# Five loads under way instead of eight, extra loads at other places, and an attention prologue in another order

## The chip, the core and the metric

The kernel runs on one core of one Trainium2 chip. The metric is the device time of one execution in microseconds (us). The core has five engines with a queue of instructions each: TensorE (PE, matmuls, with PEld for its weight loads), VectorE (DVE), ScalarE (ACT), GpSimd (POOL) and SyncE (SP). Here POOL issues nearly all loads, and SP the stores and the DMA transposes. An engine works through its instructions in the order in which the program has them, and waits on semaphores for what others produce.

## What is computed

```python
scores = (q @ k.T) / 8                       # 8 batches, 8 heads, 576 tokens, 64 columns a head
cum = cumsum(max(s, 0))                      # along the tokens
scores = where(causal, -1e9, scores + min(-(cum_i - cum_j), 0))
x = softmax(scores) @ v                      # to [8, 576, 512]
h = relu(x.T @ w_tok1) @ w_tok2              # mixes tokens, 256 hidden
u = x + h.T
out = u + relu(u @ w_ch1) @ w_ch2            # mixes channels, 1536 hidden
```

## The kernel before

The work goes batch by batch. A batch has two *quads* of four heads. For a quad, k and q are loaded with a cast to bf16 into a buffer of the ring `qkn` (five buffers), turned by PE (`tr`, L689), copied to `kT` and `qT` by ACT or DVE (L699, L701), multiplied into scores (L731), put through exp on ACT (L739) to `E`, masked on DVE (L748), and multiplied with v (L802); L831 and L835 divide by the row sums and write `x`. The bias of the reference is not added to the scores: its part that depends on the row cancels in the softmax, and the rest, a weight for each column token, is multiplied into v beforehand (`merge_v`, L631, by POOL or DVE). That weight `wT` comes from a running sum of s on DVE (`tensor_tensor_scan`, L534), an exp on ACT (L540) and a transpose on PE (L560).

Then `tok` mixes tokens (L899, L961) and writes `u` (L968), and turns it to `uT`: on PE for batches 0 and 1, by DMA transposes on SP from batch 2 on (L977). `chan` mixes channels: L1017 with the first weight, a relu on ACT or DVE (L1024, L1026), L1042 with the second, the sum with `u` (L1050) and the store on SP (L1055). While PE is at the channels of batch b, scores of batch b+1 run between.

Batch 0 is different: its causal mask is put into PSUM by a matmul of the identity with a mask (`preset`, L722) before the scores are added, where later batches mask `E` on DVE. Its first quad is loaded by SP without a cast (L518) and cast on ACT and DVE.

The order on the engines isn't written by hand. Every piece of work is an operation with engines that can do it, times, a priority and dependencies; `Plan.run` places them one after another by estimated times, and the program is emitted in the order of the planned starts. After it, `zero` matmuls (L1135) fill planned waits of PE in the first 45 us. A wait or an estimate that changes in one place can so move instructions in others.

All loads on POOL form one chain, in the order in which `load_op` is called, and the plan lets eight be under way:

```python
        if len(sent) >= 8:
            o.deps.add(sent[-8])
```

In the kernel before, POOL waits in the trace for a load to land when eight others are on their way. The order of the loads is: k and q of quad (0, 4), four pieces of v of batch 0, four loads of token weights, four of the first channel weight, quad (1, 0), two of the second channel weight, quad (1, 4), two more of the second channel weight, five pieces of v of batch 1, then for batches 2 to 7 a quad, v, and the other quad. After them come four quads that are loaded a second time: batches 0 and 1, for which only the sum of squares of q and k is taken on ACT (L647, `stage_sq`). These squares, with other sums, decide at the very end whether a slower general path runs; with these inputs it doesn't.

Of the kernel before, what the change touches and what calls it, by code (L numbers as in the profile page):

```python
# [8 lines left out]
FP32 = mybir.dt.float32  # L9
# [2 lines left out]
ALU = mybir.AluOpType  # L12


SWITCH = 0.095
STEADY = 50.0
MARGIN = 0.5
# [37 lines left out]
class Plan:  # L55
# [11 lines left out]
    def op(self, alts, reads=(), writes=(), prio=0, dma=0.0, holds=(), after=None, mode=0, lock=False, alone=None):  # L67
        o = Op()
        o.alts = alts
        o.prio = prio  # L70
        o.dma = dma
        o.mode = mode
        o.lock = lock
        o.alone = alone
        o.idx = len(self.ops)
        o.deps = set()
        o.users = []
        o.bufs = []
# [24 lines left out]
        self.ops.append(o)  # L103
        return o

    def run(self, eps=0.03):
# [11 lines left out]
        for o in ops:  # L118
            if o.nd == 0:
                for e in o.alts:  # L120
                    cands[e].append(o)
        dma_free = 6.0
        mode = 0
        order = []

# [17 lines left out]
        while left:  # L143
# [224 lines left out]
def kernel(  # L368
# [80 lines left out]
    chain = []  # L449
    sent = []  # L450

    def load_op(fn, key, us, occ=0.75, prio=-1):

        o = P.op({"POOL": (occ, 0, fn)}, writes=key, prio=prio, dma=us, after=chain[-1] if chain else None)
        if len(sent) >= 8:
            o.deps.add(sent[-8])
        sent.append(o)
        chain.append(o)

    def load_cast(n, b, h, i, src):  # L460
        def load():
            nc.gpsimd.dma_start(  # L462
                out=n.t[:, i, :, :],
                in_=src[b, h : h + 4, :, :].rearrange("(f e) (p r) d -> (e p) f (r d)", e=2, r=R))
        load_op(load, [(n, i)], 1.45, prio=-1 if b or h else -3)

    qkn = {}

# [47 lines left out]
    for ti, src in enumerate((k, q)):  # L516
# [4 lines left out]
        for f in range(2):  # L521
# [12 lines left out]
    P.op({"DVE": (1.3, 1.6, lambda: nc.vector.tensor_tensor_scan(  # L534
        out=cum[:, :], data0=one_sb[:, :], data1=s_sb[:, :], initial=0.0, op0=ALU.mult, op1=ALU.add))},
        reads=["sr"], writes=["cum"], prio=-1)
# [62 lines left out]
    def stage_v(b, cs=tuple(range(NJ))):  # L599
# [4 lines left out]
        for c in cs:  # L604
# [13 lines left out]
            load_op(load, [(vf, c)], 1.15 * n / 128, 0.92)  # L618
        if b:
            merge_v(b, cs)  # L620

# [50 lines left out]
    def quad(b, h):  # L672
# [4 lines left out]
        for ti in range(2):  # L677
# [6 lines left out]
            def tr(ti=ti, pv=pv):  # L684
                for r in range(R):
                    for e in range(2):
                        p0 = e * PR
                        for f in range(2):
                            nc.tensor.transpose(out=pv(e)[f * D : f * D + D, r * PR : (r + 1) * PR],  # L689
                                                in_=nat.t[p0 : p0 + PR, ti, f, r * D : (r + 1) * D],  # L690
                                                identity=ident[p0 : p0 + PR, p0 : p0 + PR])
            P.op({"PE": (R * 0.031, R * 0.031 + 0.21, tr)}, reads=([(nat, ti, 0), (nat, ti, 1)] if b == 0 and h == 0 else [(nat, ti)]) + ["ident"] + pads,
                 writes=[(pts[e], e) for e in range(2)], holds=[d[ti] for d in dsts], prio=(np_ - 30 * (b < 1 and h < 1), 2), mode=1)
# [13 lines left out]
    def pair(b, h, kT, qT):  # L707
# [3 lines left out]
        for pc, piece in enumerate(PIECES):  # L711
# [7 lines left out]
            if b == 0:  # L719
                def preset(ps=ps, pc=pc):  # L720
                    for hh in range(2):
                        nc.tensor.matmul(out=ps.t[:, hh * 512 : hh * 512 + 512], lhsT=ident[:, :], rhs=neg[:, pc, :],  # L722
                                         start=True, stop=False)
                P.op({"PE": (2 * c_pe(512)[0], 2 * c_pe(512)[0] + 0.21, preset)}, reads=["neg", "ident"],
                     writes=[(ps, 0)], prio=(np_ - 9, 0))

            def mm(ps=ps, cols=cols):
# [111 lines left out]
        P.op(dve(640, nrm), reads=[(pas[0], 0), (pas[1], 1), (rc, 0)], writes=[(x, h), (x, h + 2)], prio=0)  # L839

    def load_w(fn, key, us, occ=0.75):
        load_op(lambda: nc.gpsimd.dma_start(**fn()), [key], us, occ)
# [341 lines left out]
```

## Time and profile before

| | |
|---|---|
| Time, median of three runs | 304.92 us (304.0 to 306.28) |
| Time of the profiled execution | 306.06 us, span of its instructions 304.3 us |
| PE busy | 291.8 us (96%), granted clock 0.995 |
| ACT, DVE, POOL busy | 182.8, 172.0, 107.6 us |
| DMA | 39.29 MB moved, mean 129 GB/s |
| DMA queue of POOL's loads | 24.25 MB; of SP's transfers 14.44 MB |
| Chain that ended last | PE 84%, DMA 12% |

Times in the rows are counted from the span's start. "Busy" of PE includes the time in which a matmul drains while the next already runs, so consecutive matmuls overlap, and fillers count as work. An entry such as "[1.06 <-DMA uTb<-ub]" says that the engine was idle for 1.06 us before the instruction and that the landing of that DMA ended the wait; "issue" says that nothing in the profile did.

### The profile page before, as it was taken

How to read it: one execution, taken by the hardware profiler on the slowest of the kernel's cores; microseconds unless marked ns; L12 is line 12 of the kernel's file. 1: busy time of each engine (PE TensorE's matmuls, PEld its weight loads, DVE VectorE, ACT ScalarE, POOL GpSimd, SP SyncE). 2: the span in 40 equal slices, each digit the busy share in tenths (PEclk: the TensorE clock that was granted, in tenths of full speed). 3: DMA queues.
4: the chain of work that ended last, by engine and by line, in shares of the span. 5: the costliest groups of instructions: out<-in, count | busy, mean ns of one | idle time of the engine just before them, and what ended most of it. 6: DMA issues, size and time to landing. Idle time of an engine off the chain costs nothing.

```text
span 304.3 us, 8094 instructions
## 1 busy us (share of the span) xinstructions
PE 291.8 (96%) x3430; PEld 168.2 (55%) x3430; DVE 172.0 (57%) x368; ACT 182.8 (60%) x298; POOL 107.6 (35%) x147
## 2 busy tenths in 40 slices
PE   8899999899999999999999999998999999999991
PEld 3478566467754545457754545455764544457550
DVE  5962889377976456756556556956456642420030
ACT  5887884699996486609872387727761286017300
POOL 8675469999780418107620108500000000000000
PEclk9999999999999999999999999999999999999998
DMA  8999999999997673358455535894004310250032
GB/s 218 226 207 206 216 224 229 252 190 262 227 156 125 155 197 54 79 140 178 94 80 103 133 84 83 132 116 136 2 2 84 125 38 0 69 155 2 0 111 74
DMA packets 38348, 39.29 MB, mean 129 GB/s; under 512 B 17600, under 2 KB 30976, under 8 KB 38304
## 3 DMA queue, kind: packets, MB, share of 16 engines
q0 software_dynamic: 17072, 24.25, 44.6%
q1 hardware_dynamic: 21232, 14.44, 18.7%
q8 instruction: 29, 0.48, 0.7%
q14 instruction: 15, 0.12, 0.1%
HBM read 40.65 MB, written 9.44 MB: 165 GB/s over the span
## 4 chain that ended last, share of the span: by engine, by line
PE 84%; DMA 12%; POOL 1%; issue 1%; DVE 0%; POOLq 0%
PE pmx L1017 30%; PE pmx L1042 30%; PE pmx L961 5%; PE pmx L899 5%; PE psc L802 5%; PE psc L731 5%; DMA qkn<-in_k_dram 5%; PE psc L689 3%; DMA wc<-in_moe_w_ch_dram 3%; DMA vf<-in_v_dram 2%; DMA uTb<-us 2%; POOL qkn L462 1%; PE pmx L986 0%; DVE of L1050 0%; POOL keep masks.py:66 0%
## 5 line engine op out<-in xcount | busy, mean ns | idle before, releaser
L1017 PEld LDWEIGHTS <-wc 128*128 128x128 bf16 x624 | 57.9, 98 | 32.6 <-issue 1.5
L739 ACT ACTIVATE E<-psc 128x1024 bf16<-128x1024 f32 x64 | 62.2, 1024 | 22.8 <-PE psc L731 22.2
L1017 PE MATMUL pmx<-uTb,wc 128*128 128x320 bf16 (+2 forms) x384 | 56.1, 299 | 1.4 <-DMA uTb<-ub 1.1
L1042 PE MATMUL pmx<-wc,gb 128*128 128x512 bf16 (+1 forms) x252 | 55.3, 369 | 0.0
L1017 PE MATMUL pmx<-uTa,wc 128*128 128x512 bf16 (+1 forms) x240 | 45.6, 337 | 0.0
L647 ACT ACTIVATE junk<-qkn 128x1152 bf16<-128x1152 bf16 x32 | 37.3, 1166 | 11.7 <-DMA qkn<-in_q_dram 11.3
L1042 PE MATMUL pmx<-wc,ga 128*128 128x512 bf16 x192 | 44.1, 379 | 0.0
L631 POOL TENSOR_TENSOR vp<-vf,wT 128x512 bf16<-128x512 f32 (+1 forms) x31 | 32.3, 1058 | 25.6 <-PE psc L802 24.9
L1024 ACT ACTIVATE gb<-pmx 128x320 bf16<-128x320 f32 (+2 forms) x57 | 24.7, 438 | 21.2 <-PE pmx L1017 17.3
L1042 PEld LDWEIGHTS <-gb 128*128 128x128 bf16 x252 | 23.6, 98 | 24.8 <-issue 0.2
L613 POOL DMA_DIRECT2D vf<-in_v_dram x39 | 34.1, 884 | 7.3 <-DMA qkn<-in_k_dram 2.2
L748 DVE TENSOR_TENSOR E<-E,keep 128x512 bf16<-128x512 bf16 x56 | 25.8, 474 | 13.3 <-ACT E L739 13.1
L1042 PEld LDWEIGHTS <-ga 128*128 128x128 bf16 x192 | 18.2, 98 | 20.4
L1024 ACT ACTIVATE ga<-pmx 128x512 bf16<-128x512 f32 (+1 forms) x36 | 19.2, 535 | 11.7 <-PE pmx L1017 11.1
L462 POOL DMA_DIRECT2D qkn<-in_k_dram x19 | 14.1, 744 | 33.5 <-issue 31.8
L1026 DVE TENSOR_SCALAR gb<-pmx 128x320 bf16<-128x320 f32 (+2 forms) x39 | 18.8, 487 | 11.9 <-PE pmx L1017 11.5
L699 ACT COPY kT<-psc 128x576 bf16<-128x576 bf16 x22 | 13.1, 641 | 19.4 <-PE psc L689 17.9
L802 PEld LDWEIGHTS <-E 128*128 128x128 bf16 x576 | 21.1, 97 | 5.5
L835 DVE TENSOR_TENSOR x<-psc,rc 128x640 bf16<-128x640 f32 x28 | 23.0, 823 | 0.9
L1050 DVE TENSOR_TENSOR of<-pmx,ua 128x512 f32<-128x512 f32 x16 | 11.0, 689 | 19.5 <-PE pmx L1042 19.3
L731 PE MATMUL psc<-qT,kT 64*128 64x256 bf16 (+2 forms) x320 | 21.3, 250 | 0.0
L731 PEld LDWEIGHTS <-kT 64*128 64x128 bf16 x320 | 12.6, 94 | 14.6 <-issue 11.5
(107 smaller groups left out, 300.9 us busy)
## 6 DMA issues: line engine op xcount, KB each, us to landing
vf<-in_v_dram POOLq DMA_DIRECT2D x32, 256.0 KB, 7.9
out_dram<-of SPq DMA_DIRECT2D x31, 256.0 KB, 2.3
qkn<-in_k_dram POOLq DMA_DIRECT2D x19, 288.0 KB, 6.7
qkn<-in_q_dram POOLq DMA_DIRECT2D x19, 288.0 KB, 7.3
wc<-in_moe_w_ch_dram POOLq DMA_DIRECT2D x8, 384.0 KB, 11.4
out_dram<-of SPq DMA_DIRECT2D x10, 128.0 KB, 2.3
vf<-in_v_dram POOLq DMA_DIRECT2D x7, 128.0 KB, 7.4
gb<-in_k_dram SPq DMA_DIRECT2D x1, 576.0 KB, 3.9
```

Of the source, the lines that this page charges most:

```text
L613: nc.gpsimd.dma_start(out=vf.t[p0 : p0 + n, c, :, :], in_=v[b, :, c * 128 : c * 128 + n, :].rearrange("h p d -> p h d"))
L631: eng.tensor_tensor(out=vp.t[p0 : p0 + n, c, :, 0:D], in0=vf.t[p0 : p0 + n, c, :, :], in1=wT[p0 : p0 + n, cw, b * H : b * H + H].unsqueeze ...
L647: nc.scalar.activation(out=junk[:, :].rearrange("p (t n) -> p t n", t=2), in_=i, func=AF.Square, accum_out=sq[:, col : col + 1])
L731: nc.tensor.matmul(out=ps.t[:, hh * 512 + c0 : hh * 512 + c0 + e - a], lhsT=kT.t[hh * 64 : hh * 64 + 64, j0 : j0 + 128], rhs=qT.t[hh * 64 ...
L739: nc.scalar.activation(out=E.t[:, :, 512 * pc : 512 * pc + 512], in_=ps.t[:, :].rearrange("p (e n) -> p e n", e=2), func=AF.Exp, scale=0.125)
L748: nc.vector.tensor_tensor(out=o, in0=o, in1=keep[:, :].unsqueeze(1).unsqueeze(1).to_broadcast([128, 2, 2, 128]), op=ALU.mult)
L802: nc.tensor.matmul(out=o[:, ic, 0:DE], lhsT=E.t[:, hh, d0 : d0 + 128], rhs=vp.t[:, jc, h + 2 * hh, 0:DE], start=(jc == j_lo), stop=(jc == ic))
L835: nc.vector.tensor_tensor(out=x.t[:, :, :].rearrange("p c (g f e d) -> p g e f c d", f=2, e=2, d=D)[:, h // 4, h % 2], in0=pav2()[:, :, :, ...
L1017: nc.tensor.matmul(out=pm.t[:, 0 : e - a], lhsT=wc1[:, m, cc * 128 : cc * 128 + 128], rhs=uT.t[:, m, a:e], start=(m == 0), stop=(m == NMC ...
L1024: lambda cc=cc, pm=pm, a=a, e=e: nc.scalar.activation(out=g.t[:, cc, a:e], in_=pm.t[:, 0 : e - a], func=AF.Relu),
L1026: lambda cc=cc, pm=pm, a=a, e=e: nc.vector.tensor_scalar_max(out=g.t[:, cc, a:e], in0=pm.t[:, 0 : e - a], scalar1=0.0)),
L1042: nc.tensor.matmul(out=pm.t[:, na:ne], lhsT=g.t[:, cc, c * 128 : c * 128 + 128], rhs=wc2[:, cc, na:ne], start=(cc == 0), stop=(cc == NCC - 1))
```

## The change

Four things change.

1. From the seventh to the forty-fourth load, POOL copies one element of the load five places earlier into a small buffer before it issues the next (`touch`). The copy has to wait until that load has landed, so at most five are under way. From the forty-fifth on, the old rule alone holds. The plan's clock for the first DMA moves from 6.0 to 6.85, and copies of this kind get no safety margin in the plan.
2. The loads of batches 6 and 7 and the second loads of batches 0 and 1 for the squares are called in other places: behind `chan` of batch 3 come batch 6 and the squares of batch 0, behind `chan` of batch 4 batch 7 and the squares of batch 1. Ahead of each group, POOL copies one element of each transposed block of that batch's `uT`, so the group is issued only when those transposes have landed.
3. The mask presets of batch 0 depend on the first transposes (`turned`).
4. The running sum of s depends on the second transposes (those of q) and has a later priority.

In the order that the plan now makes, PE's fillers come first, then the first transposes, two presets (four matmuls), three fillers and the second transposes; the first scores stand ahead of the transposes of quad (0, 4), where they stood behind the first half of them. On DVE the sum of s stands behind a copy of q. On ACT the exp on the sum stands behind the second exp of scores instead of the first. Ahead of the k transposes of quad (1, 4) PE now has ten matmuls of L961 instead of six. The four pairs of loads for the squares move ahead of batch 7 and to its side; the last of them stands behind two products of v of batch 7 on POOL. The matmuls themselves are the same, but for the number of fillers.

```diff
+DEPTH = 5
+PACED = (6, 44)
...
-        dma_free = 6.0
+        dma_free = 6.85
...
-                    if fin > STEADY:
+                    if fin > STEADY and not u.bare:
...
+    def touch(ap, reads, col):
+        o = P.op({"POOL": (0.12, 0.2, lambda: nc.gpsimd.tensor_copy(out=seen[0 : ap().shape[0], col : col + 1], in_=ap()))},
+                 reads=reads, writes=[("seen", col)], prio=-1, after=chain[-1])
+        o.bare = True
+        chain.append(o)
+
+    probes = []
+
-    def load_op(fn, key, us, occ=0.75, prio=-1):
+    def load_op(fn, key, us, occ=0.75, prio=-1, probe=None):
+        if PACED[0] <= len(probes) < PACED[1]:
+            touch(*probes[-DEPTH], 0)
+        probes.append((probe, key))
...
-        reads=["sr"], writes=["cum"], prio=-1)
+        reads=["sr"], writes=["cum"], prio=2)
...
-            P.op({"PE": (R * 0.031, R * 0.031 + 0.21, tr)}, ...
+            turn = P.op({"PE": (R * 0.031, R * 0.031 + 0.21, tr)}, ...
+                 ... (["turned"] if b == 0 and h == 0 and ti == 0 else []) ...
+            if b == 0 and h == 0 and ti == 1:
+                scan.deps.add(turn)
...
-                P.op({"PE": (..., preset)}, reads=["neg", "ident"],
+                P.op({"PE": (..., preset)}, reads=["neg", "ident"] + ["turned"],
...
-    for b in range(2, B):
+    def stage_in(b):
         stage_qk(b, 0)
         stage_v(b)
         stage_qk(b, 4)
-    for b in range(2):
-        for h in range(0, H, 4):
-            stage_sq(b, h)
+
+    for b in range(2, 6):
+        stage_in(b)
     for b in range(B):
         for h in range(0, H, 4):
             quad(b, h)
         st = tok(b)
         chan(b, *st)
+        if b == 3 or b == 4:
+            for c in range(NJ - 1 + b % 2):
+                touch(lambda c=c, uT=st[2]: uT.t[0:1, 0, c * 128 : c * 128 + 1], [(st[2], c)], 1)
+            stage_in(b + 3)
+            for h in range(0, H, 4):
+                stage_sq(b - 3, h)
```

More of the change, by code (lines that the diff above doesn't have):

```diff
@@ L77, in op @@
         o.users = []
+        o.bare = False
         o.bufs = []
@@ L450 @@
     sent = []
-    def load_op(fn, key, us, occ=0.75, prio=-1):
+    seen = sb("seen", [128, 8], FP32, fast)
+    def touch(ap, reads, col):
[8 more added lines that the diff above has]
+        probes.append((probe, key))
         o = P.op({"POOL": (occ, 0, fn)}, writes=key, prio=prio, dma=us, after=chain[-1] if chain else None)
@@ L464, in load @@
                 in_=src[b, h : h + 4, :, :].rearrange("(f e) (p r) d -> (e p) f (r d)", e=2, r=R))
-        load_op(load, [(n, i)], 1.45, prio=-1 if b or h else -3)
+        load_op(load, [(n, i)], 1.45, prio=-1 if b or h else -3, probe=lambda: n.t[0:1, i, 0, 0:1])
     qkn = {}
@@ L533 @@
          reads=["s"], writes=["sr"], prio=-1)
-    P.op({"DVE": (1.3, 1.6, lambda: nc.vector.tensor_tensor_scan(
+    scan = P.op({"DVE": (1.3, 1.6, lambda: nc.vector.tensor_tensor_scan(
         out=cum[:, :], data0=one_sb[:, :], data1=s_sb[:, :], initial=0.0, op0=ALU.mult, op1=ALU.add))},
-        reads=["sr"], writes=["cum"], prio=-1)
+        reads=["sr"], writes=["cum"], prio=2)
     P.op(dve(1, lambda: nc.vector.tensor_scalar(
@@ L617, in stage_v @@
                 continue
-            load_op(load, [(vf, c)], 1.15 * n / 128, 0.92)
+            load_op(load, [(vf, c)], 1.15 * n / 128, 0.92, probe=lambda c=c, p0=p0: vf.t[p0 : p0 + 1, c, 0, 0:1])
         if b:
@@ L691, in tr @@
                                                 identity=ident[p0 : p0 + PR, p0 : p0 + PR])
-            P.op({"PE": (R * 0.031, R * 0.031 + 0.21, tr)}, reads=([(nat, ti, 0), (nat, ti, 1)] if b == 0 and h == 0 else [(nat, ti)]) + ["ident"] + pads,
-                 writes=[(pts[e], e) for e in range(2)], holds=[d[ti] for d in dsts], prio=(np_ - 30 * (b < 1 and h < 1), 2), mode=1)
+            turn = P.op({"PE": (R * 0.031, R * 0.031 + 0.21, tr)}, reads=([(nat, ti, 0), (nat, ti, 1)] if b == 0 and h == 0 else [(nat, ti)]) + ["ident"] + pads,
+                 writes=[(pts[e], e) for e in range(2)] + (["turned"] if b == 0 and h == 0 and ti == 0 else []), holds=[d[ti] for d in dsts], prio=(np_ - 30 * (b < 1 and h < 1), 2), mode=1)
+            if b == 0 and h == 0 and ti == 1:
+                scan.deps.add(turn)
             for e in range(2):
@@ L723, in preset @@
                                          start=True, stop=False)
-                P.op({"PE": (2 * c_pe(512)[0], 2 * c_pe(512)[0] + 0.21, preset)}, reads=["neg", "ident"],
+                P.op({"PE": (2 * c_pe(512)[0], 2 * c_pe(512)[0] + 0.21, preset)}, reads=["neg", "ident"] + ["turned"],
                      writes=[(ps, 0)], prio=(np_ - 9, 0))
@@ L841, in load_w, with probe @@
     def load_w(fn, key, us, occ=0.75):
-        load_op(lambda: nc.gpsimd.dma_start(**fn()), [key], us, occ)
+        def probe():
+            o = fn()["out"]
+            return (o[0:1, 0, 0:1] if len(o.shape) == 3 else o[0:1, 0:1])
+        load_op(lambda: nc.gpsimd.dma_start(**fn()), [key], us, occ, probe=probe)
     def load_tok():
```

## The prediction

> **What bounds the kernel now.** I read, in this order: the span, the table of busy time by stretch, the chain that ended last, and the timeline around every stretch in which TensorE (PE) is not full.
>
> ```profile
> span 304.3 us, 8094 instructions
> 50.00:60.00 10.00, 8.72 (x165) 5.65 (x163) 5.34 (x11) 5.98 (x10) 9.81 (x13) 1.00 1.09 238
> 200.00:210.00 10.00, 8.61 (x135) 4.82 (x131) 4.74 (x8) 4.50 (x8) 0.00 (x0) 1.00 1.21 171
> 210.00:220.00 10.00, 10.00 (x109) 7.38 (x107) 6.17 (x17) 7.05 (x14) 0.00 (x0) 1.00 0.01 2
> ```
>
> The second number is the stretch, the third PE's busy time in it; the last three are the granted clock, the DMA share and GB/s. From 40 to 290 us every stretch of ten reads 10.00 like the last row, but for two: 50 to 60 lacks 1.28 and 200 to 210 lacks 1.39. Before 40 the kernel has its prologue. So the kernel is bound by PE, and only three places can give time: the prologue up to about 36 us, the hole at 55 and the hole at 205. The change touches all three.
>
> **The prologue.** The rows of the timeline that set it (columns: start, time, engine, line, tile, count, idle before):
>
> ```profile
> 4.17 1.10 PE L722 MATMUL psc<-neg,ident 128*128 128x512 bf16 x4
> 8.08 1.35 DVE L534 TENSOR_TENSOR_SCAN cum<-one_sb,s_sb 64x576 f32<-64x576 f32 x1
> 8.13 1.18 ACT L699 COPY qT<-pmx 128x576 bf16<-128x576 bf16 x2 [0.88 <-PE pmx L689]
> 9.22 0.48 PE L689 MATMUL pmx<-ident,qkn 64*64 64x64 bf16 x36 [0.81 <-DMA qkn<-in_k_dram]
> 9.63 0.58 PE L731 MATMUL psc<-qT,kT 64*128 64x256 bf16 x8
> 11.65 7.11 ACT L739 ACTIVATE E<-psc 128x1024 bf16<-128x1024 f32 x7
> 13.39 3.08 DVE L631 TENSOR_TENSOR vp<-vf,wT 128x512 bf16<-128x512 f32 x5
> 17.63 1.84 PE L802 MATMUL pmx<-vp,E 128*128 128x64 bf16 x54
> 25.43 2.78 PE L1017 MATMUL pmx<-uTa,wc 128*128 128x256 bf16 x24
> ```
>
> *Presets.* The first four mask presets (1.10 us) go behind the first transposes. Five of the eight filler matmuls that stand there go, and the place that the presets leave gets fillers. Both places are waits of PE for the cast input, so I cost this at nothing; without that cover it would cost the 0.86 us that four 512-column matmuls need at 0.21 each (24 matmuls of L1042 take 5.29 in a row quoted below).
>
> *Sum of s.* The scan holds DVE from 8.08 for 1.35 us, so ACT copies both halves of qT, one after the other, to 9.31. In the changed order the scan stands behind a DVE copy of one half; both copies run at 8.13 and the longer is done near 8.9 (half of 1.18 on ACT, a little more on DVE). The first scores also move ahead of the transposes that wait for a load until 9.22. They can start near 9.0, not 9.63: first exp 0.6 us earlier. Eight exps and one smaller activation on ACT then run without a hole to 18.76, so 0.6 is the upper bound of what arrives at the MLP. Against it: the sum ends near 10.25 instead of 9.43, and the activation on it now stands behind the second exp instead of the first; 0.7 to 0.8 later, the five products with wT (3.08 us) end near 17.2 and not at 16.47, while the products with E would now start at 17.0. Gain when the channel MLP of batch 0 starts (25.43): 0.4, between 0.2 and 0.6.
>
> *The loads.* What decides at 35.5 is a load:
>
> ```profile
> 12.16 8.80 DMA wc<-in_moe_w_ch_dram
> 21.25 14.20 DMA qkn<-in_k_dram
> 33.85 1.04 PE L961 MATMUL pmx<-h,w 128*128 128x512 bf16 x4
> 35.50 0.48 PE L689 MATMUL psc<-ident,qkn 64*64 64x64 bf16 x36 [0.62 <-DMA qkn<-in_k_dram]
> 35.74 0.69 POOL L613 DMA_DIRECT2D vf<-in_v_dram  x1 [1.36 <-DMA qkn<-in_k_dram]
> 96.39 5.29 PE pmx L1042 x24
> ```
>
> The first channel weight lands at 12.16 + 8.80 = 20.96, the k of quad (1, 4), eight loads later, at 35.45: 1.81 us a load. PE waits 0.62 for it; POOL waits for it too, since eight loads are under way. The changed order puts four more matmuls of L961 (0.9 us) ahead of those transposes. PE arrives at 34.89 - 0.4 + 0.9 = 35.4. If the load still lands at 35.45, the transposes start as before with 0.9 us less work left: gain 0.9 minus whatever the load slips.
>
> Does it slip with five under way? Before load n POOL now copies one element of load n-5, so it wakes when that one has landed. The trace has no such copy; the nearest small POOL row, the 64x8 cast of wT in the next fence, takes 0.22 us. What a fresh load needs, with little ahead of it:
>
> ```profile
> 192.72 0.22 POOL L642 CAST vp<-wT 64x8 bf16<-64x8 f32 x1
> L462 POOL DMA_DIRECT2D qkn<-in_k_dram x2: 759/769/779, 171.4 to 185.0; - x2
> DMA to landing us min/median/max: 4.1/5.5/6.1
> L842 POOL DMA_DIRECT2D w<-in_moe_w_tok_dram x1: 701/701/701, 10.9 to 10.9; - x1
> DMA to landing us min/median/max: 7.4/7.4/7.4
> L613 POOL DMA_DIRECT2D vf<-in_v_dram x2: 927/1004/1082, 6.5 to 7.6; - x2
> DMA to landing us min/median/max: 8.0/8.2/8.4
> DMA to landing us min/median/max: 10.3/10.3/10.3
> ```
>
> The rows after the cast are three loads on a quiet queue, k at 171.4 (5.5), its q behind it (6.1), and k at 185.0 (4.1); then the last token weight, two pieces of v, and the v piece of 35.74 (10.3, on a full queue). Issue to landing on a quiet queue is thus 4.1 to 5.5; with 0.3 for the wait and the copy, 4.4 to 5.8. Four loads ahead at 1.81 plus the new one are 9.05 us, so the queue doesn't run dry in the long stretch. It can where two of the five are small: the token weights, of which the last lands at 10.95 + 7.4 = 18.4. In the new order it is issued when the third v piece has landed (6.5 + 8.4 = 14.9), and lands at 14.9 + 4.4 = 19.3 to 20.7, less a microsecond or so for its size: up to 1.3 late. The first channel weight waits for the fourth v piece (7.6 + 8.0 = 15.6) and lands at 20.0 to 21.4, where it landed at 20.96. Everything behind keeps the shift. Slip: 0 to 1.3; I take 0.5, since the channel weight's bounds lie around its old landing. **Prologue: 0.9 - 0.5 = 0.4 gained**, from -0.4 to 0.9. The 38 copies (8.4 us of a POOL that is busy 35%) cost nothing else: behind a waiting copy stand the next load and POOL's two products of batch 1, and PE reaches what these feed only at 47.7.
>
> The Trainium skill, page "DMA: Bandwidth & Descriptors", section "Anatomy of one DMA — SWDGE (gpsimd) path", gives a load from this queue 2.0 us plus its bytes at 436 GB/s, an estimate of 2.7 us for 288 KB; the trace's 4.1 is well above it. By the page the slip would be 0 and the sum 0.5 us better.
>
> **The hole at 55.**
>
> ```profile
> 53.73 1.07 PE L899 MATMUL pmx<-x,w 128*128 128x128 bf16 x16
> 56.08 0.38 PE L899 MATMUL pmx<-x,w 128*128 128x128 bf16 x4 [1.28 <-issue]
> q8 instruction: 29, 0.48, 0.7%
> L1055 SPq DMA_DIRECT2D out_dram<-of x1: 367/367/367, 48.4 to 48.4; - x1
> DMA to landing us min/median/max: 7.5/7.5/7.5
> L1055 SPq DMA_DIRECT2D out_dram<-of x1: 533/533/533, 236.7 to 236.7; - x1
> DMA to landing us min/median/max: 2.2/2.2/2.2
> ```
>
> PE stops for 1.28 us between the sixteenth and the seventeenth of these twenty matmuls, inside one accumulation of five, where no buffer, weight or product can be missing. "Issue" says that nothing in the profile released it. Program code itself comes over a DMA queue (0.48 MB in 29 pieces), and the hole falls where loads fill the DMA engines (238 GB/s). I read it as code that arrived late behind queued loads. That another queue's transfer does wait behind loads, the store shows: 7.5 us here, 2.2 when nothing else moves. Three loads fewer under way at 1.3 us (below) to 1.81 shorten that wait by 3.9 to 5.4 us, more than the hole. **Gain 1.28**, bounds 0 (the wait doesn't depend on the depth) and 1.28; I take the upper end, since the store's row is the nearest.
>
> The Trainium skill speaks against this: page "DMA: Bandwidth & Descriptors", section "Queues, rings and completion order", each DMA engine takes turns between the queues, packet by packet, so that the depth of POOL's queue would be nothing to another queue. By that rule the hole stays and 1.28 leaves the sum. The store's 5.3 us of extra wait doesn't agree with it well.
>
> **The hole at 205.**
>
> ```profile
> 184.03 1.03 POOL L631 TENSOR_TENSOR vp<-vf,wT 128x512 bf16<-128x512 f32 x1 [11.16 <-PE psc L802]
> 193.86 0.77 POOL L462 DMA_DIRECT2D qkn<-in_k_dram  x1 [0.92 <-ACT junk L647]
> 194.44 6.37 SPq L977 DMA_TRANSPOSE uTb<-ub  x4
> 206.54 0.70 PE L1017 MATMUL pmx<-uTb,wc 128*128 128x320 bf16 x4 [1.06 <-DMA uTb<-ub]
> DMA to landing us min/median/max: 6.6/8.7/10.5
> DMA to landing us min/median/max: 2.4/2.5/2.5
> ```
>
> The last two rows are the transposes of batch 5 (at 194) and of batch 7 (at 263): 10.5 us at worst beside the extra loads for the squares, 2.5 without. PE waits 1.06 at one place and a little at the next; the table of stretches has 1.39 in all. The change sends those loads, and the inputs of batches 6 and 7, behind one-element reads of the transposed u of batches 3 and 4, so they run between two batches' transposes; they are needed much later (batch 6 from 185, batch 7 from 220). The last pair waits for two products on POOL: 184.03 + 2 x 1.03 = 186.1, plus 0.77 for the first issue and 6.1 for the second half, 193.0, or 1.4 before the transposes begin. **Gain 1.39**, bounds 0 and 1.39. If the pair were later than that, part of the hole would stay.
>
> **Sum.** 0.4 + 1.28 + 1.39 = 3.1 off the profiled execution's own 306.06 (its span of 304.3 and 1.76 around it): 303.0. The three timed runs have a median of 304.92, 304.0 to 306.28, so the profiled one is 1.14 above it, and some executions seem to pay less for these holes already. I take 3.1 off the median, 301.8, and give 0.3 back for that: **302.1**.
>
> **The rivals.**
> *The hole at 55 stays*, there or at another place, because code waits as long behind five loads as behind eight. For it: five loads of 1.81 us keep the engines as full as eight do. Against it: the store's wait. 0.4 + 1.39 = 1.8 gained: 304.92 - 1.8 + 0.3 = 303.4. Chance 26%. (It is what the Trainium skill's section on queues would give.)
> *No slip, holes gone in full*: 0.9 + 1.28 + 1.39 = 3.6, 301.3. For it: four loads of 1.81 us cover 5.8 us of refill. Chance 18%.
> *The transposes still meet loads*: the last pair is more than 1.4 late. 0.4 + 1.28 = 1.7 gained, 303.5. Chance 6%.
> *Five loads don't keep the engines full* (slower). If the 10.3 us that the v piece issued at 35.7 needs to land were its own time and not waiting, five loads would take 10.6 us, 2.1 each. Then eight loads slip by 0.3 each to the k at 35.45, and the next eight, now 1.3 each (35.45 to 35.74 + 10.3 = 46.0), by 0.8 each: 8.7 us late in all. The products with v of batch 1 wait for the last of them; less the 0.9 and 2.7 from the two holes, 5.1 is lost: 310.0. It decides from a slip of 3.6 at 46 us. Against it are the 4.1 to 5.5 on a quiet queue. Chance 14%.
>
> **How the numbers follow.** The forecast has 36%; its own range is 301.0 to 303.4. 1% here is 3.05 us, about what a measurement of this kernel can tell from no change; the border is 301.87. Faster by over 1%: 0.45 of the forecast, nearly all of the no-slip case and a little of the others, 38%. Slower: the dry queue and a remainder for a new hole, 15%. Within: 47%. The range takes in the no-slip case and the two partial ones: 300.3 to 304.9.
>
> **What would show it.** Right: the first exp near 9.4; the k transposes of quad (1, 4) between 35.5 and 36.5; no stretch after 40 under 9.9; the transposes of batch 5 landing in about 2.5 us. Wrong: PE waiting for loads by more than a microsecond before 48 (the queue runs dry), or an "issue" hole of a microsecond anywhere (depth is nothing to code).

## The result

The changed kernel is slower. Its median is 309.72 us (308.1 to 310.03, six runs), that of the kernel before beside it 305.33 (304.0 to 306.28, six runs): ratio 1.0139, 95% interval 1.0103 to 1.0175. The forecast was 302.1, its range 300.3 to 304.9. Of the four runs of the version with three loads below, two took 318.19 and 318.38 us at a lower granted clock (0.979 and 0.974, against 0.988 and 0.990 in the other two) and are left out of its row.

Lines of the changed kernel lie some 16 to 21 lower in the file: the squares are L663 (L647 before), kT and qT copies L717, exp L757, scores L749, transposes L705, products with v L820, token MLP L920 and L982 (its relu `h` L932), channel MLP L1038 and L1063, one-element copies L458.

The span and the table of busy time by stretch of the changed kernel; the third number is PE's busy time:

```profile
span 307.5 us, 8169 instructions
20.00:30.00 10.00, 8.89 (x105) 7.58 (x101) 2.63 (x8) 7.29 (x21) 5.54 (x14) 1.00 1.16 200
50.00:60.00 10.00, 9.01 (x168) 5.86 (x167) 5.48 (x14) 5.81 (x10) 8.56 (x18) 1.00 1.06 247
140.00:150.00 10.00, 9.22 (x106) 6.66 (x101) 7.04 (x18) 7.77 (x13) 6.38 (x9) 1.00 1.12 231
150.00:160.00 10.00, 9.15 (x130) 5.50 (x129) 5.71 (x13) 8.21 (x15) 5.65 (x8) 1.00 0.79 131
190.00:200.00 10.00, 8.73 (x64) 4.34 (x63) 5.75 (x13) 9.48 (x16) 4.61 (x7) 1.00 0.46 83
200.00:210.00 10.00, 10.00 (x127) 4.98 (x128) 6.65 (x14) 1.94 (x2) 0.00 (x0) 1.00 0.51 126
```

The stretch at 200, which lacked 1.39 us before, is full. Three stretches that were full before lack 0.78, 0.85 and 1.27, the one at 50 still lacks 0.99, and the prologue has a new hole at 20 to 30. Measured at the same matmuls, PE is 0.9 us behind the kernel before from about 38 to 141 us, 4.8 behind at 193 (the first matmul of the token MLP of batch 5 starts at 192.99 instead of 188.16), and, with the hole at 205 gone, 3.2 behind at the end. What fills the new holes is in the timeline of ACT and PE, the rows of both in order of time:

```profile
143.79 1.16 ACT L663 ACTIVATE junk<-qkn 128x1152 bf16<-128x1152 bf16 x1 [1.45 <-DMA qkn<-in_q_dram]
144.96 1.92 ACT L757 ACTIVATE E<-psc 128x1024 bf16<-128x1024 f32 x2
146.01 0.70 PE L820 MATMUL psc<-vp,E 128*128 128x65 bf16 x18 [0.78 <-ACT E L757]
...
152.63 1.16 ACT L663 ACTIVATE junk<-qkn 128x1152 bf16<-128x1152 bf16 x1 [1.64 <-DMA qkn<-in_q_dram]
154.11 1.17 ACT L717 COPY kT<-psc 128x576 bf16<-128x576 bf16 x2
155.33 0.94 PE L749 MATMUL psc<-qT,kT 64*128 64x256 bf16 x10 [0.71 <-ACT kT L717]
...
188.78 1.16 ACT L663 ACTIVATE junk<-qkn 128x1152 bf16<-128x1152 bf16 x1 [1.91 <-DMA qkn<-in_q_dram]
191.23 1.16 ACT L717 COPY qT<-psc 128x576 bf16<-128x576 bf16 x2
192.44 0.62 PE L749 MATMUL psc<-qT,kT 64*128 64x256 bf16 x10 [1.27 <-ACT qT L717]
```

Each time a square (`junk`) stands in ACT's order, waits 1.45 to 1.91 us for its q to land, and holds behind it the exp or the copy for which PE then stops. These three stops are 2.8 us. The rest of the 3.9 that PE loses between 141 and 193 isn't traced in full; a part of it is in rows that run longer, such as the ten scores at 155.33, which take 0.94 us where the ten at 142.89 take 0.61. The hole at 55 has the same shape now:

```profile
52.75 1.17 ACT L663 ACTIVATE junk<-qkn 128x1152 bf16<-128x1152 bf16 x1 [7.67 <-DMA qkn<-in_q_dram]
55.20 0.36 ACT L932 ACTIVATE h<-pmx 128x256 bf16<-128x256 f32 x1
55.62 0.44 PE L920 MATMUL pmx<-x,w 128*128 128x128 bf16 x5 [0.99 <-ACT h L932]
```

In the kernel before these squares began 4.4 us earlier, and nothing in the profile released the stop at 55:

```profile
48.38 1.16 ACT L647 ACTIVATE junk<-qkn 128x1152 bf16<-128x1152 bf16 x1 [3.53 <-DMA qkn<-in_q_dram]
```

Now their q comes later, because five loads are under way and not eight, and two squares in a row run up to the relu that PE's next matmul waits for.

### The profile page after: what moved, and what is told of

Read it like the earlier page. It is cut to its first block, busy times and chain, and to the rows that moved or that the text cites. A ratio compares the mean times of both kernels' runs of the same rounds, so it can differ in the third digit from the quotient of the medians.

```text
span 307.5 us, 8169 instructions
## 1 busy us (share of the span) xinstructions
PE 294.2 (96%) x3432; PEld 168.2 (55%) x3432; DVE 172.4 (56%) x373; ACT 180.4 (59%) x292; POOL 118.1 (38%) x195
## 4 chain that ended last, share of the span: by engine, by line
PE 64%; DMA 18%; POOL 6%; DVE 5%; ACT 3%; issue 3%; SPq 0%; POOLq 0%; ACTq 0%
PE pmx L1063 25%; PE pmx L1038 22%; DMA qkn<-in_q_dram 6%; DMA wc<-in_moe_w_ch_dram 5%; DMA vf<-in_v_dram 5%; PE pmx L920 5%; PE pmx L982 4%; PE psc L820 4%; PE psc L749 3%; POOL vf L629 3%; PE psc L705 2%; POOL qkn L478 1%; DVE x L853 1%; ACT E L757 1%; DVE E L766 1%
## 5 line engine op out<-in xcount | busy, mean ns | idle before, releaser
L757 ACT ACTIVATE E<-psc 128x1024 bf16<-128x1024 f32 x64 | 62.2, 1023 | 31.8 <-PE psc L749 31.6
L1038 PEld LDWEIGHTS <-wc 128*128 128x128 bf16 x624 | 57.8, 98 | 31.6 <-issue 1.3
L1038 PE MATMUL pmx<-uTb,wc 128*128 128x320 bf16 (+2 forms) x384 | 55.9, 300 | 0.0
L1063 PE MATMUL pmx<-wc,gb 128*128 128x512 bf16 (+1 forms) x252 | 55.2, 370 | 0.0
L663 ACT ACTIVATE junk<-qkn 128x1152 bf16<-128x1152 bf16 x32 | 37.4, 1169 | 16.2 <-DMA qkn<-in_q_dram 15.9
L1038 PE MATMUL pmx<-uTa,wc 128*128 128x512 bf16 (+1 forms) x240 | 45.6, 337 | 0.0
L1063 PE MATMUL pmx<-wc,ga 128*128 128x512 bf16 x192 | 44.4, 380 | 0.2 <-DVE of L1071 0.2
L647 POOL TENSOR_TENSOR vp<-vf,wT 128x512 bf16<-128x512 f32 (+1 forms) x32 | 32.9, 1050 | 27.0 <-PE psc L820 26.6
L1063 PEld LDWEIGHTS <-gb 128*128 128x128 bf16 x252 | 23.6, 98 | 24.8 <-issue 0.4
L1045 ACT ACTIVATE gb<-pmx 128x320 bf16<-128x320 f32 (+2 forms) x53 | 22.9, 434 | 19.1 <-PE pmx L1038 15.7
L766 DVE TENSOR_TENSOR E<-E,keep 128x512 bf16<-128x512 bf16 x56 | 24.1, 436 | 17.5 <-ACT E L757 17.4
L1063 PEld LDWEIGHTS <-ga 128*128 128x128 bf16 x192 | 18.1, 98 | 20.5 <-issue 0.5
L1047 DVE TENSOR_SCALAR gb<-pmx 128x320 bf16<-128x320 f32 (+2 forms) x43 | 20.6, 487 | 11.3 <-PE pmx L1038 10.5
L1045 ACT ACTIVATE ga<-pmx 128x512 bf16<-128x512 f32 (+1 forms) x37 | 19.9, 540 | 8.8 <-PE pmx L1038 8.1
L749 PE MATMUL psc<-qT,kT 64*128 64x256 bf16 (+2 forms) x320 | 22.2, 251 | 2.2 <-ACT qT L717 1.3
L820 PEld LDWEIGHTS <-E 128*128 128x128 bf16 x576 | 20.9, 97 | 6.0 <-issue 1.0
L749 PEld LDWEIGHTS <-kT 64*128 64x128 bf16 x320 | 12.7, 94 | 17.5 <-issue 14.8
L717 ACT COPY kT<-psc 128x576 bf16<-128x576 bf16 x20 | 12.0, 643 | 15.8 <-PE psc L705 15.8
L820 PE MATMUL psc<-vp,E 128*128 128x65 bf16 x522 | 20.1, 193 | 0.8 <-ACT E L757 0.8
L920 PE MATMUL pmx<-x,w 128*128 128x512 bf16 (+2 forms) x120 | 19.6, 308 | 1.1 <-ACT h L932 1.0
```

What stands on the lines that cost most here:

```text
L647: eng.tensor_tensor(out=vp.t[p0 : p0 + n, c, :, 0:D], in0=vf.t[p0 : p0 + n, c, :, :], in1=wT[p0 : p0 + n, cw, b * H : b * H + H].unsqueeze ...
L663: nc.scalar.activation(out=junk[:, :].rearrange("p (t n) -> p t n", t=2), in_=i, func=AF.Square, accum_out=sq[:, col : col + 1])
L749: nc.tensor.matmul(out=ps.t[:, hh * 512 + c0 : hh * 512 + c0 + e - a], lhsT=kT.t[hh * 64 : hh * 64 + 64, j0 : j0 + 128], rhs=qT.t[hh * 64 ...
L757: nc.scalar.activation(out=E.t[:, :, 512 * pc : 512 * pc + 512], in_=ps.t[:, :].rearrange("p (e n) -> p e n", e=2), func=AF.Exp, scale=0.125)
L766: nc.vector.tensor_tensor(out=o, in0=o, in1=keep[:, :].unsqueeze(1).unsqueeze(1).to_broadcast([128, 2, 2, 128]), op=ALU.mult)
L820: nc.tensor.matmul(out=o[:, ic, 0:DE], lhsT=E.t[:, hh, d0 : d0 + 128], rhs=vp.t[:, jc, h + 2 * hh, 0:DE], start=(jc == j_lo), stop=(jc == ic))
```

## The experiments

Theory A: the moved loads, and the squares that read them, put ACT's in-order queue in front of PE; pacing to five adds about 1 us, mostly in the prologue; the prologue's order is worth little. Rivals: five loads under way are the whole loss (B); the wait near 28 us isn't theirs (C); five are too few anywhere (E) or only where two of them are small token weights (D); holes and clock differ between executions of one program (V); the prediction's own steps (P).

| what is different | median us | ratio to before, 95% interval |
|---|---|---|
| the changed kernel | 309.72 | 1.0139 (1.0103 to 1.0175) |
| only the moved loads | 308.97 | 1.0126 (1.0080 to 1.0171) |
| only five under way | 306.05 | 1.0030 (0.9998 to 1.0062) |
| only presets and scan | 304.78 | 0.9975 (0.9952 to 0.9997) |
| the same again, five rounds | 304.54 | 0.9968 (0.9949 to 0.9987) |
| changed, squares 8 us later | 306.85 | 1.0033 (1.0004 to 1.0062) |
| changed, squares 16 us later | 306.44 | 1.0043 (1.0013 to 1.0073) |
| changed, squares 8 later, no pacing | 305.72 | 1.0011 (0.9990 to 1.0032) |
| only moved loads, squares 8 later | 305.13 | 0.9995 (0.9973 to 1.0016) |
| five under way only from the k of batch 1 | 305.36 | 0.9994 (0.9961 to 1.0026) |
| three under way from the k of batch 2 | 309.63 and 310.45 | 1.015 and 1.017, no interval |

**Each part alone.** The diffs are against the changed kernel. Only the moved loads:

```diff
-PACED = (6, 44)
+PACED = (6, 6)
-        dma_free = 6.85
+        dma_free = 6.0
-        reads=["sr"], writes=["cum"], prio=2)
+        reads=["sr"], writes=["cum"], prio=-1)
-                scan.deps.add(turn)
+                pass
-            ... preset)}, reads=["neg", "ident"] + ["turned"],
+            ... preset)}, reads=["neg", "ident"],
```

> The kernel before with only the loads of batches 5 to 7's inputs and of the squares in their new places; no one-element copies ahead of the other loads, presets and scan as before. Theory A (the moved loads put ScalarE's squares, which wait for their q, ahead of exps and copies that TensorE needs): prologue as before, the hole at 205 gone (-1.4 to -1.6), new holes of 0.7 to 1.5 us each near 145, 155 and 191 with a square waiting for q just ahead: +2.3 us over before, 1.005 to 1.010. Rival B (the loss of the changed kernel comes from five loads under way): this kernel is 1.4 us faster than before, 0.995, and has no such holes.

The edit moves the inputs of batches 6 and 7, not of 5 to 7. Measured 1.0126, beyond the 1.010 that theory A allowed (the interval begins at 1.0080), and far from rival B's 0.995. One of its stretches, and from its timeline one stop:

```profile
150.00:160.00 10.00, 8.19 (x136) 4.94 (x136) 4.72 (x10) 8.53 (x14) 3.52 (x6) 1.00 0.67 107
```

```profile
151.44 1.16 ACT L663 ACTIVATE junk<-qkn 128x1152 bf16<-128x1152 bf16 x1 [2.58 <-DMA qkn<-in_q_dram]
154.14 0.94 PE L749 MATMUL psc<-qT,kT 64*128 64x256 bf16 x10 [1.66 <-ACT kT L717]
```

The loads of batches 6 and 7 and of the squares alone bring nearly the whole loss, with the stop near 152, a smaller one of 0.50 us near 190, and without the hole at 205 (its stretch at 200 reads 10.00). The one expected near 145 is not there in this execution.

Only five under way (both moved load groups back in their old places, the prologue as before):

> The kernel before with only the one-element copies that hold the early loads to five under way. Theory A: the k of quad (1, 4) lands about 1.3 us later than 35.45, TensorE is 0.5 to 1.0 us late from there to the end; the hole at 55 stays in some form and the hole at 205 stays: 1.002 to 1.004. Rival B: +3 us or more, 1.010. Rival P (the prediction: fewer loads shorten the wait for code): -0.8 us, 0.997, no hole at 55.

Measured 1.0030, as theory A had it; the interval just takes in no change. Against theory A, the hole at 205 did not stay (the stretch at 200 reads 9.96), though the loads stood in their old places. From the timeline, PE at the stop and POOL where the queue runs thin:

```profile
29.77 0.48 PE L705 MATMUL psc<-ident,qkn 64*64 64x64 bf16 x36 [1.08 <-DMA qkn<-in_k_dram]
...
14.38 1.65 POOL L458 COPY seen<-vf 1x1 f32<-1x1 f32 x1
16.80 0.71 POOL L863 DMA_DIRECT2D wc<-in_moe_w_ch_dram  x1
```

The first channel weight is issued at 16.80 instead of 12.16, and PE stops 1.08 us for the k of quad (1, 0); in the kernel before it had landed in time.

Only presets and scan:

> The kernel before with only the presets and the scan behind the first transposes. Theory A: whether TensorE comes to full clock at 4.4 or 7.0 us decides the first scores; if the moved presets are what keeps the clock down (a pause of TensorE before the transposes), fillers again take 427 ns up to 5 us or later and chan of batch 0 starts at 25.4 to 25.8; ratio 0.999 to 1.001. The prediction: full clock near 4.4, first exp near 9.4, chan of batch 0 at 25.0, 0.4 us faster, 0.9987.

> Only the presets and the scan behind the first transposes, again, in more rounds: 0.9952 to 0.9997 of before held in three rounds. Theory A: the first scores come 0.6 us earlier where the clock and the load of k (0, 4) let them, chan of batch 0 up to 0.4 us earlier, 0.997 to 1.000. The prediction: 0.4 us, 0.9987.

0.9975 and 0.9968: this part makes the kernel faster, by 1.0 us (0.4 to 1.6) in the longer measurement, and is the fastest version here. But not by the prediction's way: in its two profiles the channel MLP of batch 0 starts 0.7 and 1.1 us later than 25.43, with other work ahead of it, and both have a full stretch at 200. Where exactly the gain comes from stays open. Nor does this part alone bring the order that the prediction counts on. With `dma_free` at 6.0, the first scores stand behind the first transposes of quad (0, 4), as in the kernel before, and wait with them for a load; in the version with only five under way, whose `dma_free` is 6.85, they stand ahead of them. The rows of the first profile of this version, then that of the version with five under way:

```profile
9.28 0.48 PE L705 MATMUL pmx<-ident,qkn 64*64 64x64 bf16 x36 [0.76 <-DMA qkn<-in_k_dram]
9.69 0.61 PE L749 MATMUL psc<-qT,kT 64*128 64x256 bf16 x10
```

```profile
8.97 0.61 PE L749 MATMUL psc<-qT,kT 64*128 64x256 bf16 x10
```

The first exp is at 10.34 and 10.81 in the two profiles with only presets and scan, and at 9.40 with only five under way. So the earlier scores come with the part that paces the loads, not with presets and scan.

**The squares later.** Loads, copies and prologue are those of the changed kernel; only the plan's estimate of when the squares can run is 8 us later, which changes their places in ACT's order and what the plan puts around them:

```diff
-                        rdy += MARGIN_DMA if o.dma else ...
+                        rdy += MARGIN_DMA + u.late if o.dma else ...
...
-                 reads=[(n, 0), (n, 1)], writes=[("sq", col)], prio=60)
+                 reads=[(n, 0), (n, 1)], writes=[("sq", col)], prio=60).late = 8.0
```

> The changed kernel, its loads where they are, but the planner reckons ScalarE's squares 8 us later than their loads, so that they come later in ScalarE's order. Theory A: no square waits for a load, the holes at 145, 155 and 191 go and the hole at 205 stays away: 3 us less than the changed kernel, about 306.3, 1.002 to 1.005 over before. Rival B (the loads themselves, or five under way, slow the kernel): 309, no different from the changed kernel.

Measured 306.85: 2.9 us less than the changed kernel, 1.0033 against 1.0139 of before. What ACT waits for (total, times, longest) in the kernel before, in the changed kernel and in this one, then this one's stretches:

```profile
ACT junk L647 <- DMA qkn<-in_q_dram: 11.3, 4, 5.8
```

```profile
ACT junk L663 <- DMA qkn<-in_q_dram: 15.9, 7, 7.7
```

```profile
ACT junk L664 <- DMA qkn<-in_q_dram: 7.7, 1, 7.7
```

```profile
20.00:30.00 10.00, 8.29 (x91) 7.21 (x90) 2.08 (x6) 6.68 (x19) 5.65 (x15) 1.00 1.16 204
140.00:150.00 10.00, 10.00 (x115) 7.21 (x113) 5.72 (x17) 8.67 (x15) 7.50 (x11) 1.00 1.09 221
150.00:160.00 10.00, 10.00 (x151) 6.25 (x149) 6.45 (x16) 7.53 (x13) 5.68 (x8) 1.00 0.99 160
190.00:200.00 10.00, 10.00 (x70) 4.83 (x71) 6.56 (x13) 9.52 (x15) 2.15 (x4) 1.00 0.51 103
```

The three holes are gone, with the loads where they were: it is the squares' place on ACT and not the loads' traffic. The one wait of 7.7 us that is left is that of the squares near 53. The kernel before waits 11.3 us on squares too, at places where PE needs nothing from ACT; a wait costs only by what stands behind it. Without presets, scan and pacing:

> Only the moved loads, with the squares reckoned 8 us later. Theory A: against the 308.97 of the same loads with early squares, 4 us less; 0.995 to 1.000 of before. Rival B (the loads themselves delay TensorE, wherever the squares stand): 1.01.

0.9995, 3.8 us below the same loads with early squares, so rival B's 1.01 falls. Moved loads with squares placed right cost nothing, and bring nothing that can be measured either. Without the one-element copies ahead of the early loads:

> The changed kernel without the one-element copies ahead of the early loads, and with ScalarE's squares reckoned 8 us later than their loads. Theory A with the cost of five under way (about 1.7 of after_late's 1.85 us at 200 us): prologue as before or 0.3 better, no holes at 145, 155, 191 or 205; 0.994 to 0.998 of before, 303.2 to 304.4. Rival C (the wait of TensorE near 28 us has nothing to do with five loads): 306.5, like after_late.

305.72, 1.1 us below the kernel that keeps them, and its stretch at 20 is nearly whole (9.77 where the last fence has 8.29), so rival C falls:

```profile
20.00:30.00 10.00, 9.77 (x165) 7.99 (x164) 3.34 (x10) 7.17 (x20) 5.60 (x9) 1.00 1.19 207
```

But 0.994 to 0.998 was expected and 1.0011 came. The gain of the prologue's order does not add to the rest. In this version too the first scores stand behind transposes that wait for a load (first exp at 10.04). PE has no hole after 70 us in its profile, and where the expected microsecond went was not found.

Squares 16 us later:

> The changed kernel with ScalarE's squares reckoned 16 us later than their loads, in place of 8. Theory A: the squares of quad (0, 0), whose q lands near 52.7, no longer stand ahead of the activation that TensorE waits for at 55; that stop of 1.0 goes or becomes a stop of 0.2 to 0.6 released by nothing (issue); the holes at 145, 155 and 191 stay away. 0.5 to 1 us less than the 306.85 of 8 us: 1.000 to 1.003 of before. Rival: the stop at 55 is code, 1 us at the same place whatever stands on ScalarE.

```profile
50.00:60.00 10.00, 10.00 (x196) 6.75 (x193) 6.62 (x17) 6.29 (x11) 9.16 (x18) 1.00 1.06 244
```

The stop at 55 is gone, but not by the edit. The two squares ahead of the relu stand in ACT's order where they stood with 8 us; their q only landed earlier, so that they begin at 52.07 instead of 53.14 and end before PE has what the relu needs (it begins at 54.77, with 8 us at 55.59):

```profile
52.07 1.16 ACT L664 ACTIVATE junk<-qkn 128x1152 bf16<-128x1152 bf16 x1 [6.06 <-DMA qkn<-in_q_dram]
```

That fits a stop that is the squares', and no stop of another kind took its place here; it is one execution. The time is the same as with 8 us (1.0043 against 1.0033, intervals overlapping), not 0.5 to 1 us less.

**How many loads.** Five under way, but only from the k of batch 1 on (against the kernel with five throughout):

```diff
-PACED = (6, 44)
+PACED = (14, 44)
-        dma_free = 6.85
+        dma_free = 6.0
```

> The kernel before with five loads under way, but the copies begin only at the k of batch 1, behind all token weights and the first channel weights. Theory D (five run dry only where two of them are small token weights): the k of (1, 0) lands at 28.0 to 28.4 as before, no wait of TensorE near 28, 0.998 to 1.001. Rival E (five are too few anywhere, each load costs its own time beside them): the k of (1, 4) lands 1 us late or more, 1.003. Both: the hole at 55 stays.

0.9994. PE's row at the place of the stop:

```profile
28.30 0.48 PE L705 MATMUL psc<-ident,qkn 64*64 64x64 bf16 x36
```

No wait at 28: five loads of full size are enough here, and the slip comes with the copies among the token weights (theory D). The edit also sets `dma_free` back to 6.0, so the order of the first scores differs too. The runs of this kernel spread from 303.02 to 307.40 us; in two of its three profiles PE waits 1.8 and 2.3 us near 77 for masks of `E` on DVE, in the third not at all. Three loads from the k of batch 2 on (`DEPTH = 3`, `PACED = (28, 44)`):

> The kernel before with only three loads under way, from the k of batch 2 on (issued near 36 us before) to the loads of 95 us. Rival P (the prediction: code waits behind queued loads): the hole at 55 shrinks by more than 1 us, to 0.1 or less. Theory A: the hole of 0.9 to 1.2 us stays in one of the matmuls of 54 to 56. Time: 0.996 by P, 1.000 to 1.005 by A, by how late the loads of batch 2 come.

> The kernel with three loads under way from the k of batch 2 on, a second profiled execution. If fewer loads shorten the wait for code: the issue hole at 55 is 0.6 or less again. If 0.47 was chance: up to 1.5. Time 309 to 319 as before, by the loads that come late.

309.63 and 310.45 us, well above the 1.005 that theory A allowed. In the first profile PE waits 2.73 us for transposes of batch 2 (8.42 in the second, an execution of 315.46 us). SP issues them at 93.36, hardly later than in the kernel before (93.16), but now POOL issues seven loads from 90.52 to 96.2, where the kernel before issues none between 90.2 and 102.96. Beside them the transposes take 10.6 to 13.6 us to land, where they took 2.4 to 3.9:

```profile
109.53 2.95 PE L1038 MATMUL pmx<-uTa,wc 128*128 128x512 bf16 x9 [2.73 <-DMA uTa<-ua]
DMA to landing us min/median/max: 10.6/12.7/13.6
```

**The hole at 55 and the hole at 205 from one execution to the next.**

> The kernel with five loads under way from the k of batch 1 on, a second profiled execution. If fewer loads shorten the wait for code (the prediction's step): the issue hole at 55 is 0.1 to 0.6 again, below the 0.72 to 1.55 of eight loads. If 0.18 was chance: anywhere from 0.2 to 1.5.

> The same kernel, a third profiled execution, with the same two expectations.

These two executions took 307.64 and 302.76 us. The row behind the stop at 55, in the fences one after the other: only the moved loads with later squares (eight under way), five from the k of batch 1 in its first and second execution, three from the k of batch 2.

```profile
56.02 0.38 PE L921 MATMUL pmx<-x,w 128*128 128x128 bf16 x4 [1.55 <-issue]
```

```profile
55.47 0.38 PE L920 MATMUL pmx<-x,w 128*128 128x128 bf16 x4 [0.18 <-issue]
```

```profile
55.00 0.38 PE L920 MATMUL pmx<-x,w 128*128 128x128 bf16 x4 [1.07 <-issue]
```

```profile
55.45 0.38 PE L920 MATMUL pmx<-x,w 128*128 128x128 bf16 x4 [0.47 <-issue]
```

In eight profiles with eight loads under way it is 0.72 to 1.55 us (mean 1.03), with five 0.18, 1.07 and 0.52, with three 0.47 and nothing. Fewer loads go with a shorter stop on average, but 1.07 lies inside the range of eight. A piece of program code does land shortly before: the DMA table of the microsecond around it shows it, in the kernel before (from 53.6 to 54.65) and with five loads (52.95 to 53.95):

```profile
q8 instruction: 1, 0.02, 5.7%
```

```profile
q8 instruction: 1, 0.02, 6.0%
```

5.7% of 16 engines in 1.05 us and 6.0% of 16 in 1.00 are 0.96 us both: its packets took as long beside eight loads as beside five. So the depth doesn't shorten the visible transfer; whether it begins earlier for it stays open, and so does whether PE waits for it at all.

The kernel before and the changed one once more:

> The kernel before, unchanged: a second profiled execution. Theory V (the holes at 55 and 205 and the moment at which TensorE comes to full clock differ between executions of one program): the hole at 205 is anywhere from 0 to 1.6 us, as in the four kernels with unmoved loads (0, 0, 0, 0.2), the hole at 55 from 0.2 to 1.7, full clock anywhere from 4.3 to 7.0 us. The prediction: 1.39 at 205 and 1.28 at 55 again, full clock near 4.4.

> The kernel before, unchanged: a third profiled execution. The same two expectations as for the second.

They took 306.69 and 305.79 us. The stretch at 200 in them:

```profile
200.00:210.00 10.00, 8.90 (x138) 4.90 (x136) 5.31 (x9) 3.87 (x8) 0.00 (x0) 1.00 1.29 174
```

```profile
200.00:210.00 10.00, 9.79 (x144) 5.52 (x143) 5.65 (x10) 4.82 (x9) 0.00 (x0) 1.00 1.10 175
```

It lacks 1.39, 1.10 and 0.21 in three executions of one program, 0.90 in the mean, and 0 to 0.04 in seven of the eight profiles of other kernels whose loads had not been moved; in the eighth, the second with three loads, PE waits 0.72 and 0.36 for the same transposes at 216. In these seven the transposes landed slowly too, the slowest after 6.7 to 9.4 us. Those of the first profile with only presets and scan:

```profile
DMA to landing us min/median/max: 4.2/6.5/8.1
```

So loads beside the transposes make them slow, but PE stops only where the slowest takes some 9 us or more (9.4 to 10.5 in the kernel before).

> The changed kernel, unchanged: a second profiled execution. Theory A: the holes at 145, 155 and 191, behind squares that wait for their q, come again with 0.7 to 2 us each, 3 us in all; the wait for the k of (1, 0) near 29 us comes again with 1 to 2.2 us. Theory V: full clock anywhere from 4.3 to 7.0 us. If the three holes were chance, they would be elsewhere or gone.

It took 309.93 us. The three holes came again, at 145, 154 and 191 with the same rows behind squares that waited 1.67, 2.00 and 1.59 us for q; PE stopped for 1.00, 1.07 and 0.95 us. They aren't chance. The k of (1, 0) cost 0.95 again.

## Why the prediction was wrong

**The step that failed is the move of the loads.** It was costed by the transposes alone: the loads "run between two batches' transposes; they are needed much later". The input of batches 6 and 7 is. But with each pair of loads for the squares go two squares on ACT, and in the rows above nothing on ACT passes a square that waits. The prediction put this at nothing and didn't ask what is queued behind the squares. That was 3.9 us of delay (0.9 behind at 141, 4.8 at 193), 2.8 of it in the three stops, against the 1.39 gained. The moved loads alone measure 1.0126, with later squares 0.9995. The Trainium skill says in a sentence what was missed: page "PSUM — Partial Sum Buffer", section "Engine vs sequencer instructions", calls the queues of ScalarE, VectorE and GpSimd strict FIFO. The rows above agree: 1.45 to 1.91 us of a square's wait become 0.71 to 1.27 of PE's. None of the rivals had it; the slower one had another mechanism. So that a slower kernel was among them is no credit to the prediction.

**The hole at 205.** The mechanism was right as far as it goes. The transposes of batch 5 land in the forecast 2.5 us, one group for all:

```profile
L998 SPq DMA_TRANSPOSE uTb<-ub x4: 1188/1193/1196, 199.3 to 203.7; - x4
DMA to landing us min/median/max: 2.4/2.4/2.6
```

The term of 1.39 was the largest of three executions; their mean is 0.90, so some 0.5 us of the sum was never there to be gained. The 0.3 given back was for that, and too small. And seven profiles show no such hole with the loads in their old places, so moving them was not the only way to lose it.

**The hole at 55.** The term of 1.28 was wrong: a stop of 0.99 took its place, behind the squares (0.56 in the second execution). The later landing of their q was in the prediction's own arithmetic, as a slip, but only followed to PE, not to ACT. That code comes late is not settled; five loads didn't reliably take it away.

**Loads in the prologue.** The slip at the k of (1, 4) was put at 0 to 1.3, taken 0.5. The load was issued at 29.21 and took 7.5 us, so it landed near 36.7, the upper end. PE ran its transposes at 37.26, beyond the 35.5 to 36.5 forecast, but not for this load: it was still at matmuls of the token MLP, late from a stop before. The first two channel weights show why (their issues, their landings from the table of that tile, and the next stop of PE):

```profile
16.49 0.71 POOL L863 DMA_DIRECT2D wc<-in_moe_w_ch_dram  x1
17.80 0.70 POOL L863 DMA_DIRECT2D wc<-in_moe_w_ch_dram  x1
```

```profile
DMA to landing us min/median/max: 5.0/6.0/7.1
```

```profile
30.11 0.48 PE L705 MATMUL psc<-ident,qkn 64*64 64x64 bf16 x36 [1.10 <-DMA qkn<-in_k_dram]
```

They land at 21.5 and 24.9: the first at the upper bound of 21.4 that was given, the second 3.4 us behind it where 1.81 was reckoned, behind copies among the small token weights. Why the second gap is that long was not traced. And the k of quad (1, 0), three loads later, was never considered: issued at 20.97 it takes 9.1 us and lands near 30.1, 2.1 later than before (16.97 and 11.0), and there PE now stops 1.10 us. The prediction's own test, "PE waiting for loads by more than a microsecond before 48", has been met. Pacing as a whole costs 0.9 us (1.0030, just within the noise; 1.1 between the two versions with later squares), nowhere near the 310 of the slower rival.

**The sum of s and the presets.** The first exp was forecast near 9.4. With this prologue it is at 9.97 and 9.53 in the two executions of the changed kernel, and at 9.37 and 9.68 with squares 8 and 16 us later; before it is at 10.06, 10.07 and 10.47. So the order does what was said, where PE's clock lets it. That clock was the term left out, and one that neither kernel sets: the fillers behind the presets begin at 7.48, 7.04, 6.88 and 7.19, and the exp 2.49 us later each time. Little of it arrives: the channel MLP of batch 0, forecast 0.4 before 25.43, starts at 25.79, 25.27, 25.19 and 25.42.

## What to carry to other kernels

Where a load is moved, follow its consumer on the consumer's engine, not only the load's queue: ask what stands behind the instruction that will wait, and which engine needs that. When a planner places the waiting instruction by an estimated landing, that estimate has to move with the load; 8 us more of it were worth 2.9 us here. And take the size of a hole from several executions before it becomes a term: one here was 0.2 to 1.4 us in the same program.

## What the runs showed of the hardware

PE's first matmul starts at 1.21 us in the rows below, and PE comes to full clock between about 4.3 and 7.1. A 512-column matmul takes a step of 0.42 us before (seven fillers from 1.21 to 4.17) and 0.22 after (24 of them in 5.29). Four presets at full clock take 1.04, so each slow step adds some 0.2. The first four presets stand at the same place in two executions of the kernel before; the first has them nearly all at full clock, the second has none:

```profile
4.17 1.08 PE L722 MATMUL psc<-neg,ident 128*128 128x512 bf16 x4
```

```profile
4.17 1.91 PE L722 MATMUL psc<-neg,ident 128*128 128x512 bf16 x4
```

In the changed kernel two of the four presets at 6.22 still run at the slow step:

```profile
6.22 1.43 PE L740 MATMUL psc<-neg,ident 128*128 128x512 bf16 x4
```

The first scores move with it, from 8.93 to 9.54 in the four profiles with the changed prologue. The Trainium skill, page "TensorE: Matmul & The Clock Gate", section "Part 1: The HAM clock gate (the "warmup" mystery)", has this as a free-running window of some 3.4 us, whose phase differs between runs; the spread of 2.8 us here fits into one such window. The same section gives 0.5 us either way between runs, and these runs spread wider.

DMA transposes that meet loads land late: 2.4 to 3.9 us without and 10.6 to 13.6 beside them for the same batch, as the rows with three loads show.

A copy of one element on POOL takes 0.17 to 0.20 us in most rows, and took 1.65 in the row at 14.38 above, with the next load behind it.
